# Attention, Fourier mixing and FFN in one kernel: the two heads of a pair handled together after the softmax, and the transform's PSUM banks shared with the scores

## The chip, the cores and the metric

The kernel runs on one core of a Trainium2 chip. A core has TensorE (PE) for matmuls, VectorE (DVE), ScalarE (ACT), GpSimd (POOL) and SyncE (SP), which here issues nearly all DMAs. The engines run at the same time, each takes its own instructions strictly in order, and semaphores make one wait for another. Matmul results land in PSUM, which this kernel uses as eight banks of 512 fp32 values per partition. The metric is device time in microseconds; the time before is 1081.24 us, the median of three runs (1079.13 to 1081.65).

## The reference

```python
def _attn_ref(q, k, v):                      # 8 batches, 8 heads, 576 positions, 64 wide
    scores = scale * np.matmul(q, k.transpose(0, 1, 3, 2))
    scores = np.where(mask, scores + bias[None], -1e9)   # window 0 <= rel < 128, ALiBi slopes
    attn = np.exp(scores - np.max(scores, axis=-1, keepdims=True))
    attn = attn / (np.sum(attn, axis=-1, keepdims=True) + 1e-09)
    return np.matmul(attn, v)

def _moe_ref(x, w_ch1, w_ch2):               # x: the heads side by side, (8, 576, 512)
    mixed = np.real(np.fft.fft(np.fft.fft(x, axis=1), axis=2))
    u = x + mixed
    un = (u - mean(u)) / sqrt(var(u) + 1e-06)
    return u + np.maximum(un @ w_ch1, 0.0) @ w_ch2        # 512 -> 2048 -> 512
```

## The kernel before

A batch goes through three stages: attention over its 8 heads, the transform (the two Fourier transforms as matmuls with tables, and the normalisation), and the FFN. The stages of neighbouring batches overlap.

Attention takes heads in pairs: pair `p` is heads 2j and 2j+1 of batch b, with e = 0 or 1 for the head. The 576 queries are cut into five tiles `ti` of 96 to 128 rows, each against one or two blocks of 128 keys, and the tiles form three groups `i`. For a group `scores` runs the matmuls of both heads (line L403) into two PSUM tiles `sp0` and `sp1`. Then, for each head and tile, VectorE adds the bias and finds the row's extreme (L415) and ScalarE takes the exponential into a tile `P` (recorded under L169, the line of the helper `after` that runs delayed steps).

What follows differs by batch. In batches 0 and 1 (`NF` = 2) `P` is transposed on TensorE in fp32 (`turn`, L446, copied out at L449), with small matmuls on real data behind it (`warm`, L323). In batches 2 to 7 `halves` splits the `P` of one head and tile into two fp16 halves side by side, the high one on ScalarE (L428) and the low one on VectorE (a scalar_tensor_tensor `P<-P` under L169), and `flip` transposes both by one DMA on SyncE's queue (L437) into `pt`, a tile for one head and group. Here a flip means that DMA.

`values` multiplies `pt` with V into the PSUM tile `pv`, which is one bank and holds one head (L468 in fp32, L473 to L475 in halves). The order is all three groups of head 0 and then those of head 1. After each head `weigh` (L487 to L491) takes the row sums, inverts them and writes the normalised head into `X`, the batch's activations.

The transform's matmuls (`rows` L602, `middle` L619, `cols` L636) take their PSUM tile from a pool of a single bank, `pd`; in batch 0 they alternate it with the FFN's `fp`. Eight such tiles are used per batch: four of `rows`, one of `middle`, three of `cols`. The FFN's first matmul (L752) fills one of two banks `fp`; ScalarE writes its rectified high half into `hbuf` (L757), VectorE the low half (L169, `hbuf<-fp,hbuf`), and the second matmul (L767) reads them.

A fourth strand belongs to `batch_scales`: for batches 2 to 7, the q, k and v of a batch to come are read in 15 pieces (`fetch`, L273 on SyncE's queue) and squared on ScalarE (`part`, L278), which finds the largest value. For batches 3 to 7 a copy of one element on GpSimd (L272), which reads the `X` that the latest `weigh` before it in the plan has written, holds the fetch back until that `weigh` is done.

The order of the work comes from a plan: `put(t, f, ...)` places steps on a heap by planned times, in units of which 24 make a batch, and the steps are emitted in that order; the framework's scheduler then lays out each engine's own sequence. The numbers at the top of the file set the planned times.

Of the kernel before, what the change touches and what calls it, by code (L numbers as in the profile page):

```python
# [22 lines left out]
NF = 2  # L23
# [11 lines left out]
POUT = (0, 256, 0, 384, 0)  # L35
PB = 9
# [8 lines left out]
E0 = 18.423  # L45
W1A, N0 = 1.058, 20
WL = (-2.569, 0.042)
PL, VL = 8.86, 2.996
FL, SA, SD, SB, SE = 1.9, 16.181, 0.696, 24.163, 1.152
DFT = 29.394  # L50
START = 48.432
PACE, T1 = (0.447, 0.427), 13.742
SPIN, GAP = 5, 0.73
SLOW = 1.609
W2A, W2D, W2B, W2E = 13.895, 0.631, 21.285, 0.429
W1D, W1B, W1E = 0.379, 11.116, 0.508
F0 = 6.021
SW = 184
SPIN1 = 1

# [22 lines left out]
def attn_fft_ffn_kernel(  # L83
# [25 lines left out]
    ps_v, ps_d = pool("ps_v", 1, space=PSUM), pool("ps_d", 1, space=PSUM)  # L109
# [206 lines left out]
    pv = ps_v.tile([128, 512], F32, name="pv")  # L316
    spare_cols["pv"] = pv[:, 512 - SW:512]
    for _ in range(N0):
        T.matmul(pv, stack[:, 0:128], stack, start=True, stop=True)
# [67 lines left out]
    def scores(p, i):  # L387
# [19 lines left out]
        for e in range(2):  # L407
            h = 2 * j + e
            nb = small.tile([128, 5], F32, name="nb", bufs=6)
            col = 0  # L410
            for ti in grp:
                m, n, pc = TILES[ti][1], 128 * len(TILES[ti][2]), PCOL[ti]
                pt = P[e, ti] = att.tile([128, 256], F32, name="P", bufs=PB)
                tab, mul = (rel_sb, -2.0 ** -(h + 1)) if b < NF else (scs[b][2], scs[b][1][:m, h:h + 1])
                V.tensor_tensor_reduce(pt[:m, 0:n], sp[e][:m, col:col + n], tab[:m, pc:pc + n],  # L415
                                       mul, 3.0e38, ALU.add, ALU.min, nb[:m, ti:ti + 1])
                after(0.25, A.activation, pt[:m, 0:n], pt[:m, 0:n], AF.Exp, bias=nb[:m, ti:ti + 1], scale=-1.0)
                if b >= NF:
                    after(0.45, halves, p, i, e, ti)
                col += n  # L420

    def halves(p, i, e, ti):
        m, blks = TILES[ti][1:]
        n = 128 * len(blks)
        P32 = Ps[p, i][e, ti][:m, 0:n]
# [6 lines left out]
    def flip(p, i, e, ti, both):  # L432
# [46 lines left out]
    def weigh(p, e, pv):  # L479
# [14 lines left out]
        if e == 1:  # L494
            ops.pop(p)
# [439 lines left out]
```

## Time and profile before

| | |
|---|---|
| time, median of three runs | 1081.24 us |
| profiled execution, from first to last instruction | 1083.9 us (the page gives no other time for this execution) |
| PE busy | 1039.0 us, 96% |
| DVE, ACT, POOL busy | 703.2, 583.0, 48.0 us |
| mean granted TensorE clock | 0.984 |
| flips (L437) | 240, 2.4 us from issue to landing |

The profile is one execution. Busy time is the union of an engine's instructions; it leaves out waits and instructions that only issue a DMA. The idle time before an instruction is put down to what released it. A TensorE that counts as busy may still run at the lower of its two clock levels, so the granted clock is read beside it.

### The profile page before, as it was taken

The page shows a single profiled execution, that of the slowest core. Times are in us where ns is not written, and L with a number is a line of the kernel's source. Part 1 is how long each engine was busy: PE and PEld are TensorE (multiplying, and loading weights), DVE is VectorE, ACT ScalarE, POOL GpSimd, SP SyncE. Part 2 cuts the span into 40 slices and gives each one's busy share as a digit, 9 for nine tenths or more (in the row PEclk, how much of TensorE's full clock was granted, in tenths as well). Part 3 has the DMA queues.
Part 4 walks back from the last instruction along what each step waited for, and adds up shares of the span by engine and source line. Part 5 has one row for each costly group of instructions (what it writes and reads, how often), then busy time and mean ns, then how long its engine had stood idle before and what let it go on. Part 6 is the DMA issues. An engine that isn't in the chain of part 4 may idle for free.

```text
span 1083.9 us, 23935 instructions
## 1 busy us (share of the span) xinstructions
PE 1039.0 (96%) x9208; PEld 726.4 (67%) x9208; DVE 703.2 (65%) x2073; ACT 583.0 (54%) x1388; POOL 48.0 (4%) x136
## 2 busy tenths in 40 slices
PE   8998889899899999999899999999999999999998
PEld 5876776675667667675657667584757676757655
DVE  4889789687674868687674858678784836252111
ACT  6886987558444567567554556556544522241000
POOL 0000001000000000001100000001000000000000
PEclk8998989999999999999999999999999999999999
DMA  9961466727542364527643364537522330030000
GB/s 365 346 218 56 123 147 158 151 54 187 136 101 75 97 147 123 147 51 152 170 109 74 96 146 119 143 54 134 110 60 34 53 69 11 10 60 11 20 10 21
DMA packets 191506, 117.81 MB, mean 109 GB/s; under 512 B 154400, under 2 KB 164128, under 8 KB 191392
## 3 DMA queue, kind: packets, MB, share of 16 engines
q1 hardware_dynamic: 190816, 114.84, 42.4%
q8 instruction: 72, 1.18, 0.5%
q10 hardware_dynamic: 576, 1.45, 0.3%
q14 instruction: 42, 0.34, 0.1%
HBM read 70.63 MB, written 9.44 MB: 74 GB/s over the span
## 4 chain that ended last, share of the span: by engine, by line
PE 61%; DVE 16%; DMA 9%; ACT 7%; issue 3%; SPq 2%; POOL 1%; ACTq 0%; DVEq 0%; POOLq 0%
PE fp L752 25%; PE fp L767 22%; PE sp L403 4%; DMA wall<-v_dram 4%; DVE P L415 2%; DMA wall<-q_dram 2%; ACT wall L278 2%; PE pd L602 2%; PE pv L468 2%; DVE P L169 1%; PE pd L636 1%; DVE hbuf L169 1%; DMA pt<-P 1%; ACT P L169 1%; PE sp L446 1%
## 5 line engine op out<-in xcount | busy, mean ns | idle before, releaser
L767 PE MATMUL fp<-wall,hbuf 128*128 128x512 f16 x1728 | 391.2, 379 | 0.0
L752 PEld LDWEIGHTS <-wall 128*128 128x128 f16 x3840 | 338.5, 99 | 70.4 <-issue 25.2
L752 PE MATMUL fp<-uT,wall 128*128 128x256 f16 x3072 | 365.4, 275 | 20.2 <-DVE hbuf L169 11.9
L767 PEld LDWEIGHTS <-hbuf 128*128 128x128 f16 x1728 | 162.8, 98 | 184.9 <-issue 3.5
L757 ACT ACTIVATE hbuf<-fp 128x512 f16<-128x512 f32 x144 | 84.8, 589 | 202.0 <-PE fp L752 201.9
L169 ACT ACTIVATE P<-P,nb 128x256 f32<-128x256 f32 x320 | 141.9, 477 | 60.8 <-DVE nb L415 60.5
L169 DVE SCALAR_TENSOR_TENSOR hbuf<-fp,hbuf 128x512 f16<-128x512 f32 x144 | 98.8, 686 | 99.3 <-ACT hbuf L757 98.4
L169 DVE SCALAR_TENSOR_TENSOR P<-P 128x256 f16<-128x256 f32 x240 | 87.4, 391 | 40.4 <-ACT P L428 38.9
L415 DVE CUSTOM_DVE_ANT_0 P<-sp,rg,nsl 128x256 f32<-128x256 f32 x240 | 97.5, 449 | 13.7 <-PE sp L403 12.0
L278 ACT ACTIVATE wall<-wall 128x512 f32<-128x512 f32 (+2 forms) x90 | 54.4, 605 | 91.3 <-DMA wall<-k_dram 33.5
L403 PE MATMUL sp<-kk,qq 64*128 64x256 f16 (+5 forms) x880 | 95.0, 287 | 1.4 <-ACT pt L449 0.7
L428 ACT ACTIVATE P<-P 128x256 f16<-128x256 f32 x240 | 84.1, 382 | 2.4 <-DMA pt<-P 1.7
L473 PE MATMUL pv<-vhs,pt 128*128 128x65 f16 x432 | 56.0, 195 | 1.2 <-DMA pt<-P 1.1
L474 PE MATMUL pv<-vl,pt 128*128 128x64 f16 x432 | 55.9, 193 | 0.0
L169 DVE SCALAR_TENSOR_TENSOR X<-fp,misc,X 128x512 f32<-128x512 f32 x32 | 23.8, 744 | 48.4 <-PE fp L767 48.3
L475 PE MATMUL pv<-vhs,pt 128*128 128x65 f16 x432 | 55.1, 194 | 0.0
L403 PEld LDWEIGHTS <-qq 64*128 64x128 f16 (+1 forms) x720 | 32.4, 99 | 24.6 <-issue 18.8
L473 PEld LDWEIGHTS <-pt 128*128 128x128 f16 x432 | 41.0, 98 | 9.6 <-issue 1.3
L752 PE MATMUL fp<-wall,wall 128*128 128x128 f16 x768 | 46.2, 219 | 0.0
L474 PEld LDWEIGHTS <-pt 128*128 128x128 f16 x432 | 40.7, 99 | 6.1
L468 PEld LDWEIGHTS pv<-vr,pt 128*128 128x128 f32 x288 | 37.6, 199 | 6.1 <-PE pv L323 3.3
L272 POOL COPY wall<-X 1x1 f32<-1x1 f32 x75 | 26.2, 377 | 343.9 <-DVE X L491 265.0
(159 smaller groups left out, 1205.9 us busy)
## 6 DMA issues: line engine op xcount, KB each, us to landing
qr<-q_dram SPq DMA_DIRECT2D x32, 304.0 KB, 3.2
hbuf<-w_dram SPq DMA_DIRECT2D x16, 512.0 KB, 7.7
out_dram<-X SPq DMA_DIRECT2D x32, 256.0 KB, 2.2
wall<-v_dram SPq DMA_DIRECT2D x30, 256.0 KB, 3.5
vr<-v_dram SPq DMA_DIRECT2D x24, 320.0 KB, 4.1
kr<-k_dram SPq DMA_DIRECT2D x24, 289.0 KB, 3.8
wall<-q_dram SPq DMA_DIRECT2D x24, 256.0 KB, 3.0
wall<-k_dram SPq DMA_DIRECT2D x24, 256.0 KB, 3.1
```

What stands on the lines that cost most here:

```text
L169: put(now[0] + dt, lambda: f(*a, **kw))
L278: A.activation(t, t, AF.Square, accum_out=box["mx"][:, i, c:c + 1])
L403: T.matmul(sp[e][:m, col:col + n], qq[h, c0:c0 + m], keys(kk[h], ti), start=(x == 0), stop=(x == len(prods) - 1))
L415: V.tensor_tensor_reduce(pt[:m, 0:n], sp[e][:m, col:col + n], tab[:m, pc:pc + n], mul, 3.0e38, ALU.add, ALU.min, nb[:m, ti:ti + 1])
L428: A.activation(hi, P32, AF.Copy, scale=2.0 ** 14)
L468: T.matmul(pv[:, ti], pt[:, col:col + 128], ops[p][2][:, e, vc], start=first, stop=last)
L473: T.matmul(pv[:, ti], ph, vh[:, e, vc], start=first, stop=False)
L474: T.matmul(pv[:, ti, 0:D], ph, vl[:, e, vc], start=False, stop=False)
L475: T.matmul(pv[:, ti], pl, vh[:, e, vc], start=False, stop=last)
L752: T.matmul(fp[:, i * n:(i + 1) * n], w1_ap(e, c, f0 + i), uT[:, j, c, 0:n], start=(c == 0 and p == 0), stop=(c == 3 and p == 2))
L757: A.activation(ht[:, 0], fp, AF.Relu)
L767: T.matmul(op, hh[f][:, a, i * 128:(i + 1) * 128], w2_ap(e, f), start=(f == 0 and p == 0), stop=(f == 15 and p == 2))
```

## The change

Five things are changed together.

1. `P` of a tile is now one tile of 512 for both heads, in a pool of 5 in place of 9 tiles of 256. `halves` and `flip` work on both heads at once: 120 ScalarE instructions, 120 VectorE instructions and 120 flips in place of 240 each, each twice as wide.
2. `pt` is one tile per group with both heads (3 buffers of 896 in place of 6 of 448).
3. `pv` is two banks, one per head. `values` goes by groups (group 0 of both heads, group 1, group 2), and `weigh` runs once per pair: 32 times in place of 64, each over both heads.
4. The bank `pd` is gone. The transform and the small column sums (`total`) take the tiles `sp0` and `sp1` of the scores in turn, from the same four banks.
5. The numbers of the plan are others, and `values` has two tables of planned times, `VT32` and `VT16`.

```diff
-POUT = (0, 256, 0, 384, 0)
-PB = 9
+POUT = (0, 512, 0, 768, 0)
+PB = 5
-FL, SA, SD, SB, SE = 1.9, 16.181, 0.696, 24.163, 1.152
+FL, SA, SD, SB, SE = 1.598, 16.244, 0.696, 27.725, 1.152
+VT32 = (4.6, 1.989, 0.747)
+VT16 = (4.193, 1.95, 0.8)
...
-    ps_v, ps_d = pool("ps_v", 1, space=PSUM), pool("ps_d", 1, space=PSUM)
+    ps_v = pool("ps_v", 1, space=PSUM)
...
+    sides = cycle(("sp0", "sp1"))
+
+    def side():
+        return ps_s.tile([128, 512], F32, name=next(sides))
+
     def total(m):
-        sums = ps_d.tile([128, 512], F32, name="pd")[:, 0:m.shape[1]]
+        sums = side()[:, 0:m.shape[1]]
...
-    def halves(p, i, e, ti):
...
-        both = att.tile([128, 256], F32, name="P", bufs=PB).bitcast(F16)
-        hi, lo = both[:m, 0:n], both[:m, n:2 * n]
+    def halves(p, i, ti):
+        m, n = TILES[ti][1], 128 * len(TILES[ti][2])
+        P32 = Ps[p, i][ti][:m].rearrange("p (e x) -> p e x", e=2)[:, :, 0:n]
+        both = att.tile([128, 512], F32, name="P", bufs=PB).bitcast(F16)[:m, 0:4 * n]
+        pair = both.rearrange("p (e l x) -> p e l x", e=2, l=2)
+        hi, lo = pair[:, :, 0], pair[:, :, 1]
         A.activation(hi, P32, AF.Copy, scale=2.0 ** 14)
         after(0.2, V.scalar_tensor_tensor, lo, P32, 2.0 ** 14, hi, ALU.mult, ALU.subtract)
-        after(0.4, flip, p, i, e, ti, both[:m, 0:2 * n])
+        after(0.4, flip, p, i, ti, both)
...
-        if i == 0:
-            pv = ps_v.tile([128, 512], F32, name="pv")
+        if p not in pvs:
+            pv = ps_v.tile([128, 1024], F32, name="pv")
...
-        if i == 2:
-            after(0.2, weigh, p, e, pv)
+        if valued[p] == 6:
+            after(0.2, weigh, p)
...
-        V.tensor_tensor(Xs[b][:, :, h * D:(h + 1) * D], pv[:, :, 0:D],
-                        ri.unsqueeze(2).broadcast_to([128, 5, D]), ALU.mult)
+        o = 2 * D * j
+        V.tensor_tensor(Xs[b][:, :, o:o + 2 * D].rearrange("p a (e d) -> p e a d", e=2), pv[:, :, :, 0:D],
+                        ri.unsqueeze(3).broadcast_to([128, 2, 5, D]), ALU.mult)
...
     def bank(b):
-        if b == 0:
-            p = next(spare)
-            return p.tile([128, 512], F32, name="fp" if p is ps_f else "pd")
-        return ps_d.tile([128, 512], F32, name="pd")
+        if b == 0 and next(spare) == 0:
+            return ps_f.tile([128, 512], F32, name="fp")
+        return side()
...
-            put(t + (x + LC + 0.66) * f, values, p, x % 3, x // 3)
+            vt = VT32 if b < NF else VT16
+            put(t + (vt[0] + vt[1] * (x // 2) + vt[2] * (x % 2)) * f, values, p, x // 2, x % 2)
```

First place, SyncE's sequence before, in the stretch of the last pieces of q and the first of k for batch 4 (L437 is a flip, L273 a fetch):

```order
L437 DMA_TRANSPOSE pt<-P 128x4x128 x2
L169 DMA out_dram<-X 128x512
L437 DMA_TRANSPOSE pt<-P 128x4x128
L437 DMA_TRANSPOSE pt<-P 128x2x128
L437 DMA_TRANSPOSE pt<-P 128x4x128
L437 DMA_TRANSPOSE pt<-P 128x2x128
L437 DMA_TRANSPOSE pt<-P 128x4x128
L437 DMA_TRANSPOSE pt<-P 128x4x96
L273 DMA wall_109<-q_dram 128x384
L273 DMA wall_110<-k_dram 128x512
L273 DMA wall_109<-k_dram 128x512
```

The same pieces in the changed kernel (L448 is a flip, L280 a fetch, L742 the transpose of normalised activations, L176 the helper):

```order
L448 DMA_TRANSPOSE pt<-P 128x8x128
L448 DMA_TRANSPOSE pt<-P 128x4x128
L742 DMA_TRANSPOSE uT<-un 128x8x128 x2
L280 DMA wall_106<-q_dram 128x512
L176 DMA out_dram<-X 128x512
L280 DMA wall_106<-q_dram 128x384
L742 DMA_TRANSPOSE wall_107<-un 128x8x128
L448 DMA_TRANSPOSE pt<-P 128x8x128
L448 DMA_TRANSPOSE pt<-P 128x8x96
L280 DMA wall_107<-k_dram 128x512
L280 DMA wall_106<-k_dram 128x512 x2
```

Ahead of the fetch of the last piece of q there stood eight flips with one output between them; now that fetch follows another fetch and an output, and two flips stand between it and the pieces of k.

Second place, ScalarE's sequence before at the same pieces (L278 squares a piece, L757 is the rectified half that VectorE and then TensorE wait for, L378 converts q and k):

```order
L278 ACTIVATE wall_109,mx<-wall_109 128x384
L757 ACTIVATE hbuf<-fp 128x512
L278 ACTIVATE wall_110,mx<-wall_110 128x512
L278 ACTIVATE wall_109,mx<-wall_109 128x512
L757 ACTIVATE hbuf<-fp 128x512 x3
```

In the changed kernel (L285 squares a piece, L770 is the rectified half, L176 the exponential, L441 the high half of both heads):

```order
L285 ACTIVATE wall_106,mx<-wall_106 128x384
L176 ACTIVATE P<-P,nb 128x256 x2
L441 ACTIVATE P<-P 128x2x256
L285 ACTIVATE wall_107,mx<-wall_107 128x512
L285 ACTIVATE wall_106,mx<-wall_106 128x512 x2
L176 ACTIVATE P<-P,nb 128x256 x2
L176 ACTIVATE P<-P,nb 128x128 x2
L441 ACTIVATE P<-P 128x2x256
L441 ACTIVATE P<-P 128x2x128
L770 ACTIVATE hbuf<-fp 128x512 x3
```

The squares stood directly in front of rectified halves; now six exponentials and three high halves stand among the squares and between them and the next rectified half.

Third place, TensorE's sequence before, with buffer numbers, at scores of the last group of a pair in batch 3, beside the transform of batch 2 (sp0 and sp1 are the two heads' tiles):

```order
L767 MATMUL fp_4250<-wall1_110,hbuf_108 128x512
L403 LDWEIGHTS qq_3791
L403 MATMUL sp0_4418<-kk_3876,qq_3791 128x256
L403 LDWEIGHTS qq_3791
L403 MATMUL sp1_4419<-kk_3876,qq_3791 128x256
L752 LDWEIGHTS wall0_109
```

In the changed kernel head 0's scores stand here:

```order
L410 MATMUL sp0_4147<-kk_3653,qq_3576 128x256
L410 LDWEIGHTS qq_3576
L410 MATMUL sp0_4147<-kk_3653,qq_3576 128x256
L410 LDWEIGHTS qq_3576
L410 MATMUL sp0_4147<-kk_3653,qq_3576 128x256
L780 LDWEIGHTS hbuf_105
```

and head 1's some 210 rows further on, behind FFN matmuls and the `rows` tile sp1_4113 of the transform:

```order
L780 MATMUL fp_4014<-wall1_107,hbuf_105 128x512
L410 LDWEIGHTS qq_3576
L410 MATMUL sp1_4148<-kk_3653,qq_3576 128x256
L410 LDWEIGHTS qq_3576
L410 MATMUL sp1_4148<-kk_3653,qq_3576 128x256
L410 LDWEIGHTS qq_3576
L410 MATMUL sp1_4148<-kk_3653,qq_3576 128x256
L765 LDWEIGHTS wall0_106
```

The two heads' scores of this group stood side by side; now the second head's come after a tile of the transform that uses the same two banks.

## Rows read from the trace of the kernel before

**Rows 1.** The page: span, TensorE's busy time; then the clock of the core.
```profile
span 1083.9 us, 23935 instructions
PE 1039.0 (96%) x9208; PEld 726.4 (67%) x9208; DVE 703.2 (65%) x2073; ACT 583.0 (54%) x1388; POOL 48.0 (4%) x136
core 0: 1083.9 us, clock 0.984
```

**Rows 2.** Stretches: length, PE, PEld, DVE, ACT, POOL busy (count), clock, DMA share, GB/s.
```profile
0.00:76.00 76.00, 70.83 (x548) 55.00 (x548) 55.08 (x201) 58.65 (x127) 1.52 (x12) 0.96 0.90 326
76.00:163.00 87.00, 76.28 (x589) 61.15 (x588) 72.02 (x218) 73.69 (x169) 2.39 (x10) 0.88 0.43 108
163.00:285.00 122.00, 112.23 (x1030) 76.94 (x1029) 92.99 (x284) 80.00 (x200) 10.00 (x26) 0.99 0.61 140
285.00:780.00 495.00, 479.54 (x4536) 330.10 (x4534) 351.06 (x1053) 286.32 (x705) 30.24 (x77) 1.00 0.48 113
780.00:1083.90 303.90, 300.11 (x2514) 203.18 (x2511) 132.07 (x321) 84.37 (x189) 3.88 (x11) 1.00 0.17 35
281.20:284.60 3.40, 3.40 (x22) 2.46 (x20) 0.69 (x1) 0.58 (x3) 0.00 (x0) 0.50 0.70 139
```

**Rows 3.** TensorE's waits: us in total, times, longest.
```profile
PE fp L752 <- DVE hbuf L169: 11.9, 10, 2.7
PE fp L752 <- DVE X L169: 4.3, 3, 2.3
PE pd L602 <- DVE zl L610: 3.5, 3, 2.1
PE pv L323 <- DVE X L491: 2.8, 1, 2.8
PE pv L473 <- DMA pt<-P: 1.1, 1, 1.1
```

**Rows 4.** The chain of waits from 258 to 282: start, us, what.
```profile
274.47 0.42 SPq L437
...
274.99 3.91 DMA wall<-q_dram
...
278.98 0.62 ACT wall L278 x2
279.60 0.49 ACT hbuf L757
280.11 0.70 DVE hbuf L169
```

**Rows 5.** SyncE in order of time, same stretch: start, us, what.
```profile
267.12 7.77 SPq L437 DMA_TRANSPOSE pt<-P  x6
```

**Rows 6.** The two kinds of DMA transpose on SyncE: issue, ns min/median/max.
```profile
L437 SPq DMA_TRANSPOSE pt<-P x240: 1167/1202/2517, 162.9 to 877.7; - x120
```

**Rows 7.** The same of the transposes that are 1024 values wide.
```profile
L729 SPq DMA_TRANSPOSE uT<-un x32: 1231/1253/2348, 130.9 to 970.9; - x32
```

**Rows 8.** DMA issues: count, median us from issue to landing.
```profile
pt<-P SPq DMA_TRANSPOSE x240, 2.4
...
uT<-un SPq DMA_TRANSPOSE x32, 3.2
```

**Rows 9.** Groups by form: busy us, mean ns; idle before, releasers.
```profile
L169 DVE SCALAR_TENSOR_TENSOR hbuf<-fp,hbuf 128x512 f16<-128x512 f32 x144 | 98.8, 686 | 99.3 <-ACT hbuf L757 98.4
L169 ACT ACTIVATE P<-P,nb 128x256 f32<-128x256 f32 x192 | 94.4, 500 | 56.4 <-DVE nb L415 56.2
L757 ACT ACTIVATE hbuf<-fp 128x512 f16<-128x512 f32 x144 | 84.8, 589 | 202.0 <-PE fp L752 201.9
...
L169 DVE SCALAR_TENSOR_TENSOR P<-P 128x256 f16<-128x256 f32 x144 | 59.1, 419 | 31.2 <-ACT P L428 29.8
L428 ACT ACTIVATE P<-P 128x256 f16<-128x256 f32 x144 | 56.6, 403 | 1.9 <-DMA pt<-P 1.2 <-DVE P L169 0.4
...
L491 DVE TENSOR_TENSOR X<-pv,ri 128x320 f32<-128x320 f32 x64 | 31.1, 485 | 0.7
```

**Rows 10.** Page: the squares, and the one-element copies that hold fetches back.
```profile
L278 ACT ACTIVATE wall<-wall 128x512 f32<-128x512 f32 (+2 forms) x90 | 54.4, 605 | 91.3 <-DMA wall<-k_dram 33.5
...
L272 POOL COPY wall<-X 1x1 f32<-1x1 f32 x75 | 26.2, 377 | 343.9 <-DVE X L491 265.0
```

More of the change, by code (lines that the diff above doesn't have):

```diff
@@ L406, in scores @@
         P = Ps[p, i] = {}
[L407 to L413, printed above, removed]
-                tab, mul = (rel_sb, -2.0 ** -(h + 1)) if b < NF else (scs[b][2], scs[b][1][:m, h:h + 1])
[L415 to L420, printed above, removed]
@@ L422, in halves @@
-    def halves(p, i, e, ti):
-        m, blks = TILES[ti][1:]
-        n = 128 * len(blks)
-        P32 = Ps[p, i][e, ti][:m, 0:n]
-        both = att.tile([128, 256], F32, name="P", bufs=PB).bitcast(F16)
-        hi, lo = both[:m, 0:n], both[:m, n:2 * n]
+        nb = [small.tile([128, 5], F32, name="nb", bufs=6) for e in range(2)]
+        col = 0
+        for ti in grp:
+            m, n, pc = TILES[ti][1], 128 * len(TILES[ti][2]), PCOL[ti]
+            P[ti] = att.tile([128, 512], F32, name="P", bufs=PB)
+            for e in range(2):
+                h = 2 * j + e
+                pt = P[ti][:m, 256 * e:256 * e + n]
+                tab, mul = (rel_sb, -2.0 ** -(h + 1)) if b < NF else (scs[b][2], scs[b][1][:m, h:h + 1])
+                V.tensor_tensor_reduce(pt, sp[e][:m, col:col + n], tab[:m, pc:pc + n],
+                                       mul, 3.0e38, ALU.add, ALU.min, nb[e][:m, ti:ti + 1])
+                after(0.25, A.activation, pt, pt, AF.Exp, bias=nb[e][:m, ti:ti + 1], scale=-1.0)
+            if b >= NF:
+                after(0.45, halves, p, i, ti)
+            col += n
@@ new lines, in group @@
+    def group(p, i):
+        if (p, i) not in pts:
+            pts[p, i] = att.tile([128, 896], F32, name="pt", bufs=3)
+        return pts[p, i]
+    def halves(p, i, ti):
[4 more added lines that the diff above has]
+        hi, lo = pair[:, :, 0], pair[:, :, 1]
@@ L428, in halves @@
         A.activation(hi, P32, AF.Copy, scale=2.0 ** 14)
         after(0.2, V.scalar_tensor_tensor, lo, P32, 2.0 ** 14, hi, ALU.mult, ALU.subtract)
-        after(0.4, flip, p, i, e, ti, both[:m, 0:2 * n])
-    def flip(p, i, e, ti, both):
-        if (p, i, e) not in pts:
-            pts[p, i, e] = att.tile([128, 448], F32, name="pt", bufs=6).bitcast(F16)
-        o, g, m = POUT[ti], 2 * len(TILES[ti][2]), TILES[ti][1]
-        dst = pts[p, i, e][:, o:o + g * m].rearrange("p (g t) -> p g t", g=g)
+        after(0.4, flip, p, i, ti, both)
@@ L437, in flip @@
+    def flip(p, i, ti, both):
+        o, g, m = POUT[ti], 4 * len(TILES[ti][2]), TILES[ti][1]
+        dst = group(p, i).bitcast(F16)[:, o:o + g * m].rearrange("p (g t) -> p g t", g=g)
         nc.sync.dma_start_transpose(dst, both)
@@ L445, in turn @@
             for x in range(len(blks)):
-                T.transpose(tp[:, col:col + m], P[e, ti][:m, 128 * x:128 * x + 128], ident[:m, :m])
+                o = 256 * e + 128 * x
+                T.transpose(tp[:, col:col + m], P[ti][:m, o:o + 128], ident[:m, :m])
                 col += m
-        pt = pts[p, i, e] = att.tile([128, 448], F32, name="pt", bufs=6)
+        pt = group(p, i)[:, 448 * e:448 * e + 448]
         A.activation(pt[:, :col], tp[:, :col], AF.Copy)
```

49 lines of the change are left out of this document (25 added, 24 removed).

## The prediction

> **What bounds the kernel now.** I read the page first. TensorE is busy for 1039.0 of 1083.9 us; VectorE and ScalarE for 65% and 54% [rows 1]. The mean granted clock is 0.984. So the waits that TensorE shows come to 1083.9 - 1039.0 = 44.9 us, and the lower clock costs about (1 - 0.984) x 1083.9 = 17.3 us. A change that leaves TensorE's work alone moves only these 62 us. No faster ScalarE or VectorE buys anything except by way of them.
>
> Second, the stretches, to see where the 62 us lie [rows 2]. Length less busy time of TensorE gives 5.2 us before 76, 10.7 from 76 to 163 (the fp32 pairs of batch 1), 9.8 from 163 to 285, 15.5 from 285 to 780 and 3.8 after 780. The clock costs 0.04 x 76 = 3.0 us and 0.12 x 87 = 10.4 us in the first two, so 3.9 us in all the rest. From 163 to 780 the waits add up to 25.3 us: there the changed steps run in batches 2 to 7.
>
> Third, what these waits end on [rows 3]. The largest is the FFN's matmul for the low half of the rectified tile (11.9 us in ten waits, the longest 2.7); then the residual sum that frees an FFN bank (4.3), and the transform's bank `pd`, single, until VectorE has drained it (3.5 in three, so 1.2 each). A wait for the normalisation to free `pv` occurs once, with 2.8. For a flip TensorE waited once, 1.1 us.
>
> Fourth, why the rectified tile is late. The chain from 258 to 282 runs backwards from it like this: high half on ScalarE, before it two squares of fetched pieces, before these the fetch, 3.91 us on the way, and before that a flip on SyncE [rows 4]. SyncE had been issuing six flips in a row for 7.77 us when the fetch's turn came [rows 5]. ScalarE takes its work in order, so a square whose piece has not arrived holds up the rectified tile behind it. The squares show 91.3 us of idle ScalarE before them, nearly all for DMAs [rows 10]. And after the 2.7 us wait, the clock stands at 0.50, the lower level, from 281.2 to 284.6 [rows 2]: 1.7 us more. That is the pattern I take for most of the waits from 163 to 780: flips, then fetch, square, rectified tile, TensorE.
>
> **Part by part.** TensorE's work is unchanged: the same matmuls, in another order. Nothing is gained or lost there directly.
>
> Flips. One takes 1202 ns of SyncE's queue [rows 6]. A transpose of 1024 values, as wide as the merged flips of most tiles, takes 1253 [rows 7]: the issue hardly grows with width. So 240 x 1.202 = 288 us of SyncE become 120 x 1.253 = 150, 138 less. Landing grows from 2.4 to 3.2 us [rows 8]. The six flips that took 7.77 us would be three and take some 3.9, and the fetch behind them would go out about 4 us earlier: more than the 2.7 us wait at its end. As bounds for a merged issue I keep 1.2 us and twice that; by the latter SyncE gains nothing.
>
> The Trainium skill (DMA: Bandwidth & Descriptors, "Issuing engines are not separate DMA queues") says that the time a sequencer needs to start a DMA is usually small beside the DMA. Here it is 1.2 us against 2.4 to landing [rows 6, 8], half of it, so the trace does not agree for transposes. By the rule, fewer issues would buy nothing and the gain below would be 0; the sum goes by the row.
>
> Halves. The high half of 256 takes 403 ns on ScalarE, the low one 419 on VectorE [rows 9]. For 512 the bounds are the same time again and double. The nearest rows are the rectified halves, 589 and 686 ns at 512 [rows 9]; I take those. Two merged into one save 2 x 403 - 589 = 217 and 2 x 419 - 686 = 152 ns; over the 72 merged pairs of the main form that is 15.6 us of ScalarE and 10.9 of VectorE, and if the other 96 instructions gain as much each, 26 and 18. Both engines have idle time, so this counts only as shorter queues in front of the rectified tiles.
>
> Normalisation. The multiplication over 320 takes 485 ns [rows 9], 64 times. For 640 I add 320 values at the VectorE slope (686 - 419) / 256 = 1.04 ns and get 819 (bounds 485 and 970): 32 x (970 - 819) = 4.8 us. Its small companions are halved as well. One `weigh` per pair in place of two also halves the occasions on which `pv` must be drained before the next values; against that, both heads now wait for the last one's matmuls.
>
> Fetches. Each piece from batch 3 on is held by a copy that reads the latest normalised `X`; GpSimd's idle time before the copies ends on that for 265.0 us [rows 10]. With one `weigh` per pair the pieces behind one are more, but the plan places them later after it, and the order on ScalarE puts more work between the squares and the next rectified tile: at the place shown six exponentials and three high halves, about 6 x 500 + 3 x 589 = 4.8 us where none stood [rows 9]. That is as much as a fetch in flight takes.
>
> `pt`. A group's buffer is now free one group earlier in relation to its next use, since values go by groups. TensorE's waits on flips are 1.1 us [rows 3], so that buys at most 1 us; I count 0.
>
> Wider pieces. Head 0 now waits for head 1: one exponential (500), the wider halves (589 - 403 and 686 - 419) and the longer landing (0.8 us), together 1.75 us later per group [rows 8, 9]. TensorE waits for a flip once in the whole trace, so the matmuls stand far enough behind; I count 0, and up to 1.75 us for each of 72 groups if that cover is gone.
>
> Shared banks. Eight transform tiles per batch, 64 in all, leave the single bank for the scores' four. The wait for `pd` (3.5 us) should go. But scores now queue for banks that a transform tile holds: at the third place of the order, head 1's scores of a group come some 210 rows after head 0's. Nothing before shows such a wait; the nearest is the 1.2 us for `pd`. I take two of them in the sum, and bound it by none and by three per batch.
>
> The sum, against the profiled execution's 1083.9 us: the three kinds of wait that end on late rectified tiles, FFN banks and `pd` are 11.9 + 4.3 + 3.5 = 19.7 us, of which I let two thirds go, 13.1; half of the 3.9 us of clock outside the first 163 us, 2.0; of the one wait for `pv`, 1; new waits for shared banks +2.4. Together -13.7. The first 163 us I leave as they are: their waits hang on weights, fp32 transposes and VectorE at 72 of 87 us busy, of which the change takes little. 1083.9 - 13.7 = 1070.2; the runs' median lies 2.7 us under this execution, so 1067.5, and I say 1067 us.
>
> **The rivals.** *All of the middle clears* (12%): the waits from 163 to 780 (25.3 us) and the clock's 3.9 go together, since one hangs on the other: 1081 - 29 = 1052 us. For it: the chains there look alike. Against it: a fetch still takes 3.9 us and is still held by `weigh`.
>
> *The relief stays off the path* (12%): SyncE, ScalarE and VectorE get shorter queues, but the late squares were due to the gate on `weigh` and the landing, which remain, and a shorter lead (`FL` x `SE` falls from 2.19 to 1.84 units) eats the rest: 1081 us, within 3. For it: 265 us of copies waiting for `X` [rows 10].
>
> *The shared banks bind* (10%): three transform tiles of each batch make TensorE wait, or delay the scores by as much: 24 x 1.2 = 29 us in place of the 2.4 counted, and two more falls of the clock, 3.4: 1067 - 2 + 29 + 3 = 1097 us, slower. It decides against the change from 13 tiles on (13.7 + 2.4 = 16 us at 1.2). For it: the order, and that scores start everything else in attention. Against it: four banks in place of one, and the wait for `pd` is short today.
>
> *The wider pieces come too late* (4%): the 1.75 us of a group show at TensorE once in six groups, 12 x 1.75 = 21 us: 1067 + 21 = 1088 us. The trace speaks against it with its single wait of 1.1 us [rows 3]. The Trainium skill (Perfetto Trace Analysis, "Optimizing Scalar/DVE Operations") advises for this very state, ScalarE and VectorE not saturated but causing gaps elsewhere, to break instructions up so that work completes sooner; this change merges them. By that rule the time would be the 1088 us. No row shows it yet.
>
> **How the numbers follow.** My forecast has 62%; its own range is 1057 to 1078. A measurement here can tell about 0.3%, 3.2 us, from no change. Faster: 0.62 + 0.12 = 0.74; the same: 0.12; slower: 0.10 + 0.04 = 0.14. The range of 8 in 10 runs from 1053 (most of the first rival is at or below it) to 1084, which takes in the second rival and leaves both slower ones out.
>
> **What would show it.** Right, if TensorE's idle time falls from 45 to about 31 us and mostly between 163 and 780; if the waits for the rectified tile shrink to about 4 us, ScalarE's idle time before squares falls well below 91 us, and flips are 120 with an issue near 1.25 us and a landing near 3.2; if the wide halves take near 589 and 686 ns. Wrong, if squares wait as long as now, if scores or transform tiles show waits on drained banks of more than a few us, or if values wait for flips. It also fails if the stretch before 163 us changes by more than some 5 us either way, since I count nothing there.

## The result and the profile after

The changed kernel takes 1092.2 us (median of four runs, 1089.4 to 1097.0) against 1080.2 for the kernel before beside it: a ratio of 1.0121, 95% interval 1.0088 to 1.0154, some 13 us slower. The forecast was 1067 (1053 to 1084), faster.

The page's head and the core's clock, after (to be read against [rows 1]):

```profile
span 1091.2 us, 23153 instructions
PE 1036.4 (95%) x9208; PEld 726.3 (67%) x9208; DVE 683.4 (63%) x1857; ACT 574.0 (53%) x1268; POOL 46.0 (4%) x136
core 0: 1091.2 us, clock 0.972
```

VectorE's busy time fell by 19.8 us (some 23 counted) and ScalarE's by 9.0 (16 to 26 counted). TensorE's idle time rose from 44.9 to 54.8 us, and its clock fell. The stretches of [rows 2], and a last one for the longest stretch in which TensorE stands still, called the hole below (length, then busy time and count of PE, PEld, DVE, ACT, POOL, clock, DMA share, GB/s):

```profile
0.00:76.00 76.00, 61.51 (x512) 49.13 (x512) 57.22 (x191) 55.51 (x122) 1.52 (x12) 0.94 0.86 323
76.00:163.00 87.00, 79.54 (x573) 61.63 (x574) 60.66 (x168) 68.89 (x152) 2.46 (x9) 0.81 0.32 84
163.00:285.00 122.00, 110.39 (x989) 74.89 (x986) 89.86 (x262) 80.09 (x187) 8.95 (x28) 0.97 0.66 152
285.00:780.00 495.00, 477.95 (x4560) 330.93 (x4557) 342.62 (x938) 282.92 (x631) 29.23 (x76) 0.99 0.49 113
...
66.10:78.40 12.30, 0.00 (x0) 0.00 (x0) 12.12 (x39) 6.62 (x13) 0.00 (x0) 0.69 0.23 82
```

Before 76 us TensorE has 14.5 us idle in place of 5.2; from 163 to 780 it has 28.7 in place of 25.3, so the middle did not clear either. TensorE's waits (us in total, times, longest), against [rows 3]:

```profile
PE pv L487 <- DMA pt<-P: 18.8, 8, 4.8
PE fp L615 <- ACT fh L588: 12.3, 1, 12.3
PE fp L765 <- DVE hbuf L176: 6.1, 8, 1.6
PE sp L410 <- DVE nb L423: 3.1, 4, 1.4
PE fp L780 <- DVE hbuf L176: 2.0, 1, 2.0
```

The rectified tile costs 8.1 us (11.9 before), the waits for `X`, `pd` and the drained `pv` are gone. Two new ones are larger than all of these: values wait 18.8 us for flips, and the first matmul of transform 0 waits 12.3 us in one piece for its folds (the sums and differences in which VectorE and ScalarE prepare a transform's input). The sizes of the changed instructions (busy us, mean ns; then flips' issue, ns min/median/max, and landing; then the squares of fetched pieces), against [rows 6, 8, 9, 10]:

```profile
L441 ACT ACTIVATE P<-P 128x512 f16<-128x512 f32 x72 | 44.6, 620 | 0.5
L176 DVE SCALAR_TENSOR_TENSOR P<-P 128x512 f16<-128x512 f32 x72 | 49.3, 684 | 33.2 <-ACT P L441 32.5
L506 DVE TENSOR_TENSOR X<-pv,ri 128x640 f32<-128x640 f32 x32 | 26.2, 819 | 0.4
```
```profile
L448 SPq DMA_TRANSPOSE pt<-P x120: 1197/1233/2685, 180.3 to 881.7; - x120
...
pt<-P SPq DMA_TRANSPOSE x120, 3.3
```
```profile
L285 ACT ACTIVATE wall<-wall 128x512 f32<-128x512 f32 (+2 forms) x90 | 54.5, 606 | 65.2 <-DMA wall<-v_dram 30.3 <-DMA wall<-k_dram 25.8 <-DMA wall<-q_dram 8.5
```

Every size came out near the forecast (620, 684, 819 ns, 1233 ns, 3.3 us for 589, 686, 819, 1253, 3.2), and ScalarE idles 65.2 us before squares in place of 91.3. Size was not the error.

### The profile page after: what moved, and what is told of

The parts are those of the page before. It is cut to its first block, busy times and chain, and to the rows that moved or that the text cites. A ratio compares the mean times of both kernels' runs of the same rounds, so it can differ in the third digit from the quotient of the medians.

```text
span 1091.2 us, 23153 instructions
## 1 busy us (share of the span) xinstructions
PE 1036.4 (95%) x9208; PEld 726.3 (67%) x9208; DVE 683.4 (63%) x1857; ACT 574.0 (53%) x1268; POOL 46.0 (4%) x136
## 4 chain that ended last, share of the span: by engine, by line
PE 71%; DVE 15%; DMA 5%; ACT 5%; issue 3%; SPq 0%; POOL 0%; DVEq 0%; ACTq 0%; POOLq 0%
PE fp L780 27%; PE fp L765 26%; PE sp L410 5%; PE pv L481 3%; PE sp L615 2%; DMA pt<-P 2%; DVE P L423 2%; ACT P L176 2%; DVE P L176 1%; DVE hbuf L176 1%; PE sp L458 1%; PE sp L649 1%; DVE st L722 1%; PE pv L330 1%; DMA wall<-k_dram 1%
## 5 line engine op out<-in xcount | busy, mean ns | idle before, releaser
L770 ACT ACTIVATE hbuf<-fp 128x512 f16<-128x512 f32 x144 | 84.6, 589 | 200.8 <-PE fp L765 200.8
L176 ACT ACTIVATE P<-P,nb 128x256 f32<-128x256 f32 (+2 forms) x320 | 137.6, 477 | 67.9 <-DVE nb L423 66.5
L176 DVE SCALAR_TENSOR_TENSOR hbuf<-fp,hbuf 128x512 f16<-128x512 f32 x144 | 98.4, 684 | 102.1 <-ACT hbuf L770 102.0
L423 DVE CUSTOM_DVE_ANT_0 P<-sp,rg,nsl 128x256 f32<-128x256 f32 (+2 forms) x240 | 97.3, 451 | 37.7 <-PE sp L410 35.1
L410 PE MATMUL sp<-kk,qq 64*128 64x256 f16 (+5 forms) x880 | 91.8, 290 | 3.1 <-DVE nb L423 3.1
L176 DVE SCALAR_TENSOR_TENSOR P<-P 128x512 f16<-128x512 f32 (+2 forms) x120 | 73.4, 629 | 33.9 <-ACT P L441 33.1
L285 ACT ACTIVATE wall<-wall 128x512 f32<-128x512 f32 (+2 forms) x90 | 54.5, 606 | 65.2 <-DMA wall<-v_dram 30.3
L487 PE MATMUL pv<-vhs,pt 128*128 128x65 f16 x432 | 53.9, 197 | 18.8 <-DMA pt<-P 18.8
L176 DVE SCALAR_TENSOR_TENSOR X<-fp,misc,X 128x512 f32<-128x512 f32 x32 | 23.9, 746 | 68.6 <-PE fp L780 67.4
L441 ACT ACTIVATE P<-P 128x512 f16<-128x512 f32 (+2 forms) x120 | 65.9, 575 | 0.6
L487 PEld LDWEIGHTS <-pt 128*128 128x128 f16 x432 | 40.9, 98 | 30.9 <-DMA pt<-P 21.6
L489 PE MATMUL pv<-vhs,pt 128*128 128x65 f16 x432 | 53.5, 195 | 0.0
L410 PEld LDWEIGHTS <-qq 64*128 64x128 f16 (+1 forms) x720 | 32.4, 100 | 22.2 <-issue 18.5
L488 PEld LDWEIGHTS <-pt 128*128 128x128 f16 x432 | 40.8, 99 | 5.7
L481 PE MATMUL pv<-vr,pt 128*128 128x65 f32 x288 | 41.8, 287 | 0.1
L489 PEld LDWEIGHTS <-pt 128*128 128x128 f16 x432 | 41.0, 98 | 0.4 <-issue 0.2
```

The source lines that it names most:

```text
L176: put(now[0] + dt, lambda: f(*a, **kw))
L285: A.activation(t, t, AF.Square, accum_out=box["mx"][:, i, c:c + 1])
L410: T.matmul(sp[e][:m, col:col + n], qq[h, c0:c0 + m], keys(kk[h], ti), start=(x == 0), stop=(x == len(prods) - 1))
L423: V.tensor_tensor_reduce(pt, sp[e][:m, col:col + n], tab[:m, pc:pc + n], mul, 3.0e38, ALU.add, ALU.min, nb[e][:m, ti:ti + 1])
L481: T.matmul(pv[:, ti], pt[:, col:col + 128], ops[p][2][:, e, vc], start=first, stop=last)
L487: T.matmul(pv[:, ti], ph, vh[:, e, vc], start=first, stop=False)
```

## What the runs were to tell apart

The change has four parts that can be separated: shared banks, values by groups in two banks, merged pieces, and new numbers in the plan. The theories after the result: *opening* (transform 0 stands too early in TensorE's order), *flips* (values are asked for too soon after merged, later pieces), *shared banks*, and, later, *transform 0 in the ring*, a sharper form of the first and third. The ring is the four banks of the tiles `sp0` and `sp1`, two for each name, which go round among the users of that name.

All ratios are to the kernel before, run beside it; intervals are about 0.3% to either side, 3 us, so a difference of two ratios is good to some 5 us. The last four columns are from the profiled executions: how many us later than before a kernel had begun 7, 15 and 25% of TensorE's matmul work, and the end of it (each matmul weighted with its duration at the upper clock; the kernel before is there at 72, 176, 292 and 1079 us). The order of work differs between kernels, and with other weights the lags at 7 to 25% move by up to some 10 us, so they show where a large loss lies and no more. A profiled execution is also one execution: that of the kernel before (a span of 1083.9 us, so a time of about 1086, since the times of other runs are 2 us above their spans) is some 5 us above its median, that of e9 is the slowest of seven (1094.2 us for a median of 1085.2), that of e10 the fastest of six (1116.1 for 1120.6). For the whole time the ratio counts.

| kernel | us | ratio | 7% | 15% | 25% | end |
|---|---|---|---|---|---|---|
| changed | 1092.2 | 1.0121 | +17.6 | +3.6 | +10.0 | +7.3 |
| e1 opening numbers of before | 1105.6 | 1.0235 | +29.6 | +17.8 | +22.3 | +17.7 |
| e2 values 0.607 later | 1092.7 | 1.0113 | +17.5 | +6.2 | +12.8 | +7.6 |
| e18 values 0.307 later | 1090.8 | 1.0098 | +17.4 | +6.1 | +13.0 | +3.8 |
| e4 narrow pieces | 1112.6 | 1.0302 | +18.2 | +4.8 | +13.9 | +26.4 |
| e5 before + shared banks | 1129.7 | 1.0433 | +37.4 | +34.0 | +44.2 | +46.9 |
| e6 e5 + values by groups, pairs weighed once | 1120.4 | 1.0353 | +30.6 | +18.6 | +25.0 | +35.2 |
| e7 e6 + merged pieces | 1109.6 | 1.0259 | +30.3 | +18.4 | +28.8 | +24.7 |
| e9 before, transforms 1-7 share | 1085.2 | 1.0070 | -1.3 | +4.2 | +5.4 | +8.3 |
| e10 before, transform 0 shares | 1120.6 | 1.0384 | +19.7 | +10.4 | +37.9 | +29.9 |
| e13 before + merged pieces | 1077.5 | 0.9982 | +2.4 | +2.6 | +0.3 | -8.4 |

## Experiments: the numbers of the plan and the values' times

**Opening numbers (e1).**

```
-PACE, T1 = (0.433, 0.273), 13.371      +PACE, T1 = (0.447, 0.427), 13.742
-F0 = 5.72                              +F0 = 6.021
-W1D, W1B, W1E = 0.737, 9.954, 0.638    +W1D, W1B, W1E = 0.379, 11.116, 0.508
(E0, PL, SA, W2A, W2D, W2B and transform 0's time likewise)
```

> The changed kernel with the opening numbers of the kernel before (pace of the first batch and of its transform, weight times, first feed-forward), values and everything of the steady batches as changed. Theory 'opening' (transform 0 stands too early in TensorE's order, so TensorE waits 12.3 us for its folds and loses clock twice): the hole at 66 to 78 us falls below 3 us, the lag at 176 us goes from 3.6 to about 0, and the time falls from 1092 to 1080 - 1089. Theory 'flips' (the loss is values that come too early behind the transposes): the hole may go, but the time stays within 1088 - 1094 because the 18.8 us of values waiting for flips remain with the three stretches at half clock. Theory 'shared banks': no change beyond 3 us.

It went the other way: 1105.6 us, and flips still cost 16.0 us. The new opening numbers are no cause of the loss; they make good 12 us of it. The theory 'opening', as a fault of the numbers, falls.

**Later values (e2, e18), and both (e3).**

```
-VT16 = (4.193, 1.95, 0.8)
+VT16 = (4.8, 1.95, 0.8)      # e18: 4.5; e3: 4.8 and e1's numbers
```

> The changed kernel with the fp16 values asked for 0.607 of a unit later (4.8 in place of 4.193 units of about 4.87 us behind a pair's first scores, so some 3 us later in TensorE's order), all else as changed. Theory 'flips': the 18.8 us that values wait for transposes fall below 5 us, the falls of the granted clock at 220, 432 and 678 us go, and the time falls by 12 to 25 us, to 1067 - 1080. Theory 'opening': the flips' waits fall too, but the time only by 0 to 6 us. Rival 'later values only move the wait': TensorE then waits as long for the rectified tile or the drained value banks, and the time stays within 3 us of 1092.

> The changed kernel with the fp16 values 0.307 of a unit later (4.5) and nothing else. Values 0.607 later left the time as it was; 0.307 later took 14 us off where transform 0 stood in the feed-forward's banks (1099.1 to 1085.2). Theory 'early values have a price of their own, and 0.607 overshoots into waits for the rectified tile': 1076 - 1084. Theory 'the wait only moves': within 4 us of 1092.

> Both: the opening numbers of the kernel before and the values 0.607 of a unit later. If the two losses stand apart and add up, the time is the changed kernel's less both single gains: 1055 - 1075, faster than either kernel. If one loss hides the other, it is no better than the better of the two single edits.

e2 takes 1092.7 us, e18 1090.8, e3 1110.1 (1.0271, no better than e1). TensorE's waits in e2, and in e18:

```profile
PE fp L765 <- DVE hbuf L176: 12.4, 5, 6.0
PE fp L615 <- ACT fh L588: 12.3, 1, 12.3
PE pv L487 <- DMA pt<-P: 5.2, 5, 2.6
PE sp L615 <- ACT fh L588: 4.7, 2, 2.5
```
```profile
PE fp L765 <- DVE hbuf L176: 12.8, 8, 6.3
...
PE sp L615 <- ACT fh L588: 6.0, 2, 3.1
...
PE pv L487 <- DMA pt<-P: 3.9, 2, 2.0
```

Of 18.8 us of waiting for flips 13.6 and 14.9 are gone; in their place stand 10.6 us (e2) and 15.0 (e18) more for rectified tiles, folds and drained score banks (in e18 5.1 us after 3.1). The largest wait on the page cost no time that can be measured: it was where TensorE met a lateness that it otherwise meets elsewhere. 'Flips' falls, and the rival written beside it holds. What makes a flip late can be read at the second longest of these waits, 4.6 us at 433 us. The rows (start, us, engine, line, what) are the low half that the flip transposes, SyncE's order, GpSimd's copies, and the transfer:

```profile
424.54 0.67 DVE L176 SCALAR_TENSOR_TENSOR P<-P 128x512 f16<-128x512 f32 x1
...
425.28 2.81 SPq L280 DMA_DIRECT2D wall<-v_dram  x2
428.19 0.38 SPq L339 DMA_DIRECT2D qr<-q_dram  x1
428.66 0.38 SPq L340 DMA_DIRECT2D kr<-k_dram  x1
429.15 7.24 SPq L448 DMA_TRANSPOSE pt<-P  x2
...
424.13 1.13 POOL L279 COPY wall<-X 1x1 f32<-1x1 f32 x1 [4.49 <-ACT wall L285]
425.63 2.11 POOL L279 COPY wall<-X 1x1 f32<-1x1 f32 x1 [0.38 <-ACT wall L285]
...
429.15 4.27 DMA pt<-P
```

The half was ready at 425.2 us, but its flip stands on SyncE behind two fetches of `v`, which GpSimd's copies hold until 425.3 and 427.7 us, and behind two loads; it goes out 3.9 us late, at 429.15, and the transfer is the last 4.27 us. At the longest wait, 4.8 us at 681 us, the same order stands ahead of the flip, with the same 3.9 us. In these two places the fetches that the change was to relieve hold up the flips.

**Narrow pieces (e4).**

```
-                after(0.45, halves, p, i, ti)        # both heads at once
+                    after(0.45, halves, p, i, e, ti) # each head, 240 halves and flips
```

> The changed kernel with halves and transposes made for each head alone again (240 halves and 240 transposes per kind and engine as before, in the changed banks, order and times). Theory 'width' (the merged piece waits for both heads and lands late, 3.3 against 2.4 us): values' waits for flips fall from 18.8 below 9 us and the time falls by 8 us or more. Theory 'times' (values are asked for too early, whatever the width): they stay at 14 us or more, and 120 more issues of 1.2 us on SyncE and 120 more instructions each on ScalarE and VectorE make the time the same or up to 15 us longer (1090 - 1107).

1112.6 us, 20 more than with merged pieces and beyond either forecast; flips still cost 22.7 us (15.7 and 7.0 on its two lines). In the changed kernel merging is a gain, so 'width' falls. The Trainium skill (Perfetto Trace Analysis, "Optimizing Scalar/DVE Operations") says that, where ScalarE and VectorE are not saturated but cause gaps on other engines, breaking instructions up may let work be completed sooner. This case does not agree: e4 breaks them up, and the flips with them, and takes 20 us more.

## Experiments: the change rung by rung

**Shared banks alone (e5), values by groups (e6), merged pieces (e7).**

```
e5, in the kernel before:
-    sums = ps_d.tile([128, 512], F32, name="pd")[:, 0:m.shape[1]]
+    sums = side()[:, 0:m.shape[1]]
-    return ps_d.tile([128, 512], F32, name="pd")      # bank(b)
+    return side()
e6: the changed kernel (one normalisation for a pair) with e4's narrow pieces, all numbers of before but VT16
e7: the changed kernel, all numbers of before but VT16
```

> The kernel before with one edit: the transform's tiles and the sums share the scores' two names of banks, and the bank of their own is given up; nothing else, every number of the plan as before. Theory 'shared banks bind': TensorE's scores wait for drained banks (now 0.3 to 0.9 us apiece) or the transform does, and the time rises by 6 to 16 us to 1087 - 1097, most of what the change lost. Theory 'order' (the loss stands in when values and transform 0 are asked for): within 3 us of 1081.

> Next rung: shared banks, values in two banks by groups at the changed times (4.193, 1.95, 0.8), one normalisation for a pair, but narrow pieces for each head and every other number of the plan as before. Theory 'values by groups are early': 8 to 14 us of values waiting for flips and a time 15 to 30 us above the rung before (1096 - 1112). Theory 'numbers of the opening and the steady batches': without the new numbers this rung is within 5 us of the rung before.

> Next rung: the changed kernel whole, with every number of the plan before put back except the times of the values. Theory 'width gains': merged pieces take 15 to 20 us off the rung before, as they did with the changed numbers (1112.6 without them, 1092.2 with). Theory 'width is worth nothing here': within 5 us of it. Between this rung and the changed kernel stand the numbers alone: if they gain what the opening numbers alone gained (13 us), this rung comes to 1105; if the steady numbers lose that again, to 1092.

With before at 1080 the ratios make +46.8 us for sharing, -8.7 for values by groups, -10.1 for merged pieces and -14.9 for the new numbers: +13.1. Each step is good to some 5 us and holds for this order of the rungs; the step to e6 also has one normalisation for a pair, tiles of 512 for `P`, one `pt` tile per group and the times of `VT32`. 'Shared banks' was right in kind and three times too low in size, 'values by groups are early' was wrong. All of e5's loss but 13 us is there at 15% of the work.

**Which transform (e9, e10).**

```
e9:   bank(b): transforms 1 to 7 take side(); transform 0 and the sums keep ps_d
e10:  bank(0): the tiles that took ps_d take side(); all else keeps ps_d
```

> The kernel before with transforms 1 to 3 alone in the scores' banks; transform 0 and the sums keep the bank of their own. Theory 'transform 0 is in the ring': sharing all of it cost 47 us, 38 of them ahead of 163 us, because the tiles of one name are handed out in the order in which the steps are planned, so the scores planned behind transform 0 stay behind it in TensorE's order; without transform 0 in the ring there are as many scores ahead of its first matmul as before, and the time is 1083 - 1093, 9 us at most for the steady batches. Rival 'any transform in the score banks blocks': three transforms cost at least as much as the one, 1110 - 1130.

> The complement: in the kernel before, only those of transform 0's tiles that had the bank of their own (every third of its eight) go into the scores' banks; transforms 1 to 3 and the sums keep theirs. Theory 'transform 0 is in the ring': 25 to 45 us above the kernel before (1106 - 1128), with a hole of 5 us or more ahead of its folds and 20 us or more at half clock ahead of 163 us. Rival: within 10 us of 1081.

+0.70% and +3.84%: together 4.5%, e5 has 4.33%. So in the kernel before the sums cost nothing that can be measured. The expectation of e9 speaks of transforms 1 to 3, but there is one transform per batch, and the edit moves all seven behind the first: six matmuls per transform have this form, and 42 of them run in the ring.

```profile
L607 PE MATMUL sp<-tab_sb,stack x42: 285/287/287, 200.6 to 942.5; 128*128 128x289 f16 x42
```

These seven, with 56 tiles, cost some 7 us; transform 0 costs some 41, through three tiles of its eight. TensorE at the place in e10 (start, us, line, operation, count, idle before it and its releaser):

```profile
84.88 0.16 PE L624 MATMUL sp<-a,tab_sb 128*128 128x1 f16 x1 [14.17 <-DVE a L594]
84.97 2.07 PE L408 MATMUL sp<-kk,qq 64*128 64x256 f32 x4
```

A one-column matmul of `middle` waits 14.2 us for a fold, with scores right behind it that need no fold. How many score matmuls ran ahead of transform 0's first matmul, in before and in e10 (count; ns; first and last start):

```profile
L403 PE MATMUL sp<-kk,qq x128: 269/376/792, 7.5 to 89.6; 64*128 64x256 f32 x76, 64*128 64x128 f32 x28, 64*96 64x256 f32 x24
```
```profile
L408 PE MATMUL sp<-kk,qq x88: 269/376/789, 8.3 to 61.3; 64*128 64x256 f32 x52, 64*128 64x128 f32 x20, 64*96 64x256 f32 x16
```

128 against 88; the same count is 128 in e9 and 88 in e5, e1 and the changed kernel. Of 160 fp32 score matmuls the last starts at 126.6 us before and at 166.3 in the changed kernel. The mechanism that I read from the code: the two banks of a name go round in the order in which steps are planned, so scores planned behind a tile of transform 0 can't be laid out ahead of it, and wait with it for VectorE's folds. It fits 128 and 88, though a count is good to a few only (124 in e13, which shares nothing). What the runs show is that the tiles in the ring take 40 score matmuls and the time with them. TensorE then runs at the lower clock (stretch 76 to 163, e5 and e10; 0.88 in [rows 2]):

```profile
76.00:163.00 87.00, 74.22 (x410) 56.78 (x409) 47.19 (x158) 53.77 (x130) 1.80 (x6) 0.62 0.27 75
```
```profile
76.00:163.00 87.00, 73.65 (x534) 56.78 (x533) 66.84 (x184) 63.52 (x141) 1.82 (x6) 0.77 0.30 81
```

VectorE is busy 47 to 67 of 87 us, less than before (72): over the stretch it has less to do while scores are missing. The clock of this stretch alone is no measure: e9 shows 0.80 there.

In e10 the hole is only part of the loss. By the lags 10 us of it are there at 15% of the work and 38 at 25%, and in between TensorE waits once more, up to 297 us, for transposed activations:

```profile
PE fp L757 <- DMA uT<-un: 13.1, 1, 13.1
```

In e5, which has 34 us at 15%, no such wait is seen. How it follows from the late scores is not shown.

## Experiments: remedies in the changed kernel

**Transform 0 later (e8), out of the ring (e11), with later values (e12), sums out too (e14).**

```
e8:   transform_of(0): PACE[0] * DFT + 1.5, first feed-forward left in place
e11:  bank(b): if b == 0: all eight tiles from ps_f
e12:  e11 and VT16 = (4.5, 1.95, 0.8)
e14:  e12 and total(): ps_f.tile(...) in place of side()
```

> The changed kernel with transform 0 planned 1.5 units later and the first feed-forward left at its time, nothing else. Theory 'opening': the 12.3 us that TensorE waits for transform 0's folds at 66 to 78 us fall below 5 us, one of the two stretches at half clock ahead of 140 us goes, and the time falls by 4 to 12 us to 1080 - 1088. Theory 'the hole is filled again later' (VectorE and ScalarE bound the opening, TensorE has the same work left behind the hole): within 3 us of 1092.

> The changed kernel with all eight tiles of transform 0 in the feed-forward's two banks (before: six of the eight), so that none of them stands among the scores' tiles; all else as changed. Theory 'transform 0 is in the ring': more scores go ahead of its first matmul, the hole of 12.3 us falls below 4 us, the stretch ahead of 163 us gains 4 to 15 us, and the time is 1077 - 1088. Rival 'the feed-forward's banks block instead' (W2's sums and the first feed-forward wait for transform 0's tiles): a new wait on fp of 5 us or more ahead of 163 us and a time within 4 us of 1092 or above it.

> The same, and the fp16 values 0.307 of a unit later (4.5 in place of 4.193), half as far as the 0.607 that took the flips' waits from 18.8 to 5.2 us but left the time at 1092.7. If the best point lies between, flips below 10 us and the rectified tile below 10 us, and 3 to 8 us less than the run before it; if the wait only moves from one to the other, within 3 us of it.

> The changed kernel with transform 0 and also the four kinds of sums in the feed-forward's banks, values 0.307 of a unit later as in the run at 1085.2. If the sums in the score ring (waits of 2.7 and 3.4 us at 129 and 136 us, 17 us at half clock behind them) were what is left of the loss ahead of 163 us, the lag of 8 us at 184 us falls below 3 and the time to 1077 - 1082; if VectorE's late work sets it whatever the bank, within 3 us of 1085.

e8: 1091.7 us (1.0084). The hole is broken up: a wait of 7.1 us at 77 us, with three of 1.7 to 2.1 us within 10 us of it. By the ratios that is 4 us less than the changed kernel, no more than the intervals allow. e11 (before, five of the eight tiles stood there, not six as its expectation says): 112 score matmuls go first and the hole is gone, but the time is 1099.1 (1.0179). At 7% it is level with before (-0.7 us) and by 11% it is 17.1 late:

```profile
PE sp L161 <- DVE wm L222: 3.5, 1, 3.5
PE sp L458 <- DVE nb L423: 3.5, 1, 3.5
```

Both stand at 123 to 135 us, and from 127 us on 17 us run at the lower clock: a sum, in the score ring, waits at 127 us for the maximum of weights on VectorE (the last such sum ran at 123 us before). e14 differs from e12 in the sums alone, which leave the ring too. The last of the 160 fp32 score matmuls then starts at 114 us in place of 160 in e12, so here the sums do hold scores up. e14 is 9.7 us ahead of before at 11%; then the first feed-forward waits 14.8 us for its transposed activations, and the time is 1098.9 (1.019). e12: 1085.2 (1.0068). So scores that run early are not enough: each removal let the next wait through, and no remedy by banks alone made the changed kernel faster. That e12 is 14 us under e11, where the same shift gave 1.4 on the changed kernel (e18), is not explained; the lags put 12 us of it between 15 and 25% of the work.

## Experiments: merged pieces without shared banks

**Merged pieces in the kernel before (e13), new fetch times (e15), later first feed-forward (e16, e17).**

```
-PB = 9, P tiles of 256, pt tiles of 448 for each head
+PB = 5, P tiles of 512, pt in one tile per group (768 x2, 896, 512)
 halves and flip for both heads as in the change; values head by head in one bank as before
 (an all-zero row of the transform's table is left out of memory to make room)
e15: e13 and FL = 1.598, SB = 27.725    e16: e15 and F0 = 6.35    e17: e15 and F0 = 6.8
```

> The kernel before with the merged pieces alone: halves and transposes for both heads at once (120 of each less), P in tiles of 512, transposed P in one tile for each group (two for the first group, one for each other). Values stay head by head in one bank, the transform keeps its bank, every number of the plan is as before. Theory 'the forecast's mechanism holds by itself' (half as many flips and halves relieve SyncE and ScalarE, and the loss came with the shared banks): waits for the rectified tile and for X, together 16.2 us before, fall below 9 us, and the time falls to 1062 - 1075, faster than both kernels. Rival 'merged pieces pay only where values come by groups': values wait for flips or flips for their single tiles, and the time stays within 5 us of 1081.

> The first of these three with the fetch and square times of the changed kernel (1.598 and 27.725 in place of 1.9 and 24.163 units). If the new times suit the merged pieces, 2 to 8 us below the first; if they were suited to the changed banks alone, the same within 3 us or slower.

> The kernel before with merged pieces and the changed fetch times (the run at 1075.4), and the first feed-forward planned 0.33 of a unit later (6.35 in place of 6.021), because its first matmul waits 6.3 us at 137 us for the transposed activations of batch 0. If that wait is lost time, 2 to 6 us less, 1069 - 1073; if scores and values that come in its place only run into VectorE's queue, within 2 us of 1075.

> The same with 0.78 of a unit (6.8). If the wait of 6.3 us is gone at 6.35 already, no better than that run, and up to 5 us slower where the feed-forward's work is missing as cover.

e13: 1077.5 against 1078.8, ratio 0.9982 (0.9962 to 1.0001), the rival's result. TensorE's waits in it, and two stretches:

```profile
PE fp L762 <- DMA uT<-un: 6.6, 1, 6.6
PE pv L483 <- DMA pt<-P: 4.8, 4, 2.2
PE fp L762 <- DVE hbuf L173: 4.7, 5, 1.3
PE sp L454 <- ACT P L173: 3.7, 3, 1.8
PE fp L777 <- DVE hbuf L173: 3.3, 2, 1.8
PE pd L612 <- ACT fh L585: 3.0, 2, 1.9
```
```profile
163.00:285.00 122.00, 112.76 (x1046) 75.48 (x1044) 95.41 (x279) 82.32 (x188) 12.31 (x26) 1.00 0.63 150
285.00:780.00 495.00, 485.86 (x4595) 334.05 (x4593) 352.91 (x994) 283.00 (x629) 24.69 (x77) 0.99 0.52 116
```

The waits that the forecast named shrink as it said (rectified tile 11.9 to 8.0, `X` 4.3 to 0.6), and idle time from 163 to 780 falls from 25.3 to 18.4 us. But 6.6 us of waiting for transposed activations have come at 140 us, 4.8 for flips, 3.0 for folds; all idle time is 43.8 us after 44.9. The profiled execution shows 8 us less than that of before, the medians 1 to 2; I go by the medians.

e15: 1075.4 (0.9963, interval 0.9939 to 0.9987). e16: 1076.8 (0.9980), its wait for activations still 5.5 us. e17: 1069.7 us, ratio 0.9922 (0.9895 to 0.9949), faster than both kernels. Its wait for activations is 6.4 us all the same, so it is not faster for the reason in its expectation; its profiled execution, the slowest of its eight, is only 1 us under e15's, and why e17's runs are 5 us shorter stays open.

## Why the prediction was wrong

**Shared banks, the step that failed.** It was priced at "two of them", 2 x 1.2 = +2.4 us, from the wait for `pd`. In the kernel before, sharing by itself costs 47 us; 59 tiles move into the ring (not 64, since five of transform 0's stay with `fp`), and three of them make 41 of the 47. The row priced how long a bank takes to drain; the cost was what is queued behind a tenant that is late for its own inputs. Waits on drained banks are small to the last (3.1 us on `sp L410` after). The prediction showed head 1's scores displaced in the order and still counted drains. This is shown by adding the sharing to the kernel before; taking transform 0 out of the ring of the changed kernel (e11) did not win the time back, and only with later values (e12, 1.0068) is part of it gone.

**The first 163 us left as they are.** Transform 0 runs there and was part of the shared banks; 41 of the 47 us come from it, though in e10 much of that shows only after 176 us. Its own warning ("fails if the stretch before 163 us changes") was the right place to look, and the order of instructions at 66 to 91 us shows 88 scores for 128.

**The clock, -2.0.** It went the other way: by the prediction's formula it costs (1 - 0.972) x 1091.2 = 30.6 us in place of 17.3. Of these 0.06 x 76 + 0.19 x 87 = 21.1 lie before 163 us, which leaves 9.5 in place of 3.9.

**Two thirds of 19.7 us, -13.1.** The waits went nearly as said, but the time did not: -2 us by medians in the kernel before (e13), -10 where the banks are shared (e6 to e7), -20 with the changed numbers (e4 to changed). The prediction let two thirds of these waits go without naming what would be late next in their place; e13 names it.

**Numbers, not priced.** The plan's new numbers take 15 us off (e7 to changed), 12 of them in the opening (e1). That they suit a structure that is late there is my reading; no run puts them into the kernel before. **Values by groups** were counted at -1 for `pv` and 0 for `pt`; the step that brings them with narrow pieces (e6) gives -9. **Wider pieces** were counted at 0 because the matmuls stood far enough behind their flips; values now wait 18.8 us for flips, but taking these waits away won nothing.

**Rivals.** 'The shared banks bind' (10%, 1097) named the resource, with the wrong place (three tiles in each batch; transforms 1 to 7 cost 7 us in all) and price; that 1097 lies 5 us from the measured 1092 is luck, since +47 and -34 stand behind it. The 1088 of the next rival lies as near. 'The wider pieces come too late' had its sign fulfilled, values wait for flips, and is refuted all the same: e2 and e18 take the wait away and win nothing, e4 takes the width away and loses 20 us. The Trainium skill (DMA: Bandwidth & Descriptors, "Issuing engines are not separate DMA queues") says that the time to start a DMA is usually small beside the DMA itself. The prediction drew from it that fewer issues buy nothing. Halves and issues together, halved in number, bought 2 us in the kernel before (e13), near that, and 10 to 20 in the changed banks; no run halves the issues alone.

## What to carry to other kernels

Before two users are put in one ring of banks, ask not how long a tile takes to drain but how late its inputs come and what must stand behind it in the order; count, at the place, how much independent work now runs ahead of it. A wait in the list is a price only if the time falls when it is taken away: here some 14 us of waiting went twice, and the time stayed. Where a change carries both structure and retuned numbers, build the rungs between, since the numbers can hide most of what the structure costs.

## What was not expected of the hardware

The transposes came as the rows had it: twice the width costs SyncE 1233 ns in place of 1202, and lands after 3.3 us in place of 2.4. Not expected was this: in the changed kernel the clock stood at 0.50, the lower level, from 118.5 to 135.6 us although TensorE shows no gap in that stretch:

```profile
118.50:135.60 17.10, 17.10 (x69) 12.74 (x68) 6.77 (x29) 13.95 (x31) 0.00 (x0) 0.50 0.32 66
```

Single waits of 0.4 and 0.6 us at 115 and 117 us are all the idle time of some size that went before. TensorE counts as busy throughout, so idle time shows nothing of this loss; by the two levels it is an estimated 8.6 us of work at the upper clock, half of 17.1.
